# Reordering one stretch of a fused attention and FFN kernel: the halves of the first attended sums ahead of one exponential and one scaling, and a row block's low halves behind a transposition

## The chip, the cores and the metric

The kernel runs on one core of a Trainium2 chip. The metric is device time of one execution in microseconds. A core has several engines that run their own instruction queues side by side: TensorE (PE, matrix products), VectorE (DVE), ScalarE (ACT), GpSimd (POOL) and SyncE (SP, used here to issue DMAs). They wait for one another through semaphores. Within one engine, instructions run in the order in which the compiler queued them.

## The reference

Two branches read the same 2048 x 512 input and are mixed by a gate per row, all in float32.

```python
# attention branch, 32 heads of width 16
q, k, v = split(x @ wqkv)
pq, pk = q @ w_phi[h], k @ w_phi[h]
phi_q = concat(softmax(pq), softmax(-pq))
phi_k = concat(softmax(pk), softmax(-pk))
kv, z = phi_k^T v, sum_s phi_k
a = (phi_q kv) / (phi_q z + 1e-6) @ wo
# feed-forward branch, hidden width 1792
b = relu(x @ w1 + b1)**2 @ w2 + b2
# gate
g = sigmoid(sum(x * gate_w))
out = g * a + (1 - g) * b
```

## The kernel before

Every float32 product is made of three faster ones: each operand is split into a rounded high half and the remainder, its low half, and `mm3` (L74) adds high by high, high by low and low by high. So each operand needs two operations before TensorE can use it: ACT copies it to the high half, and DVE subtracts that from the source to get the low half (`split`, L61; the subtraction is L66 in the profile, the copy L63).

The rows are worked in four blocks of 512, each of four chunks of 128. The feed-forward branch goes over the blocks twice, with one half of the hidden width each time (7 of the 14 tiles). That makes 56 items (`work_list`, L889). An item is an "up" product with its relu, square and split (`up`, `hidden`), and, two items later (`LAG`), the four "down" products that use it (`down`). This stream never ends from the first to the last microsecond, and the attention is fitted between its products: during the first pass over the blocks the keys and values are summed up; during the second the queries are worked, two chunks (a pair) at a time.

The order of the work around the change is written out by hand: `at(slot, f, ...)` puts a step into a slot, and the main loop runs item t with the slots 2t, 2t + 0.5 (in the middle of the up product), 2t + 1 and 2t + 1.5 (in the middle of the down products). The steps of query chunk n are:

- `do_q` (L767): the product q of the chunk on TensorE; then `q_exps` (L361) with `exps` (L329): DVE takes the largest and smallest of each head (mx, mn, L337 and L338) and subtracts them (e, L339 and L340), here called the spread; ACT takes the exponential (L342); DVE sums it (sm, L324) and takes a reciprocal (r, L326); POOL multiplies the exponentials by the normalizers (ez, L367).
- `do_phi` (L770): `q_phi` (L370) sums ez on DVE (dz, L377), works a short chain of small operations (den and w, L378 to L385) and scales the exponentials (`scaled`, L347). `transposed` (L391) transposes the result on DVE (tb, L393) and issues twelve DMAs that carry its pieces to their places in phiT (L403); the other four pieces are copied on ACT (`diagonal`, L409).
- `do_n` (L778) with `numer` (L415): when both chunks of a pair are in phiT, TensorE makes their attended sums (num, L420), and ACT and DVE split those into halves (o).
- `finish` (L811) with `attended` (L441): the product of o with wo (att), added to the row on DVE (L819).

Two means bend the order that the compiler's scheduler gives each engine, which otherwise goes by the place in the program and by what it reckons to be ready. `tc.high_priority(offset=AHEAD)` treats instructions as if they stood 150 places earlier. `tc.issue_after(i)` puts the instructions of the block that run on i's engine behind i in that engine's queue; it does not bind other engines.

`do_x` (L627) with `load_x` (L110) loads and splits a row block of the second pass: the high halves are copied on ACT (xh), the low halves subtracted on DVE (xl). It runs at slot 61 for the block that TensorE first reads in slot 66, and again at slots 72 and 82. Chunk 0 and chunk 1 (the first pair) are worked from slot 56.5 on, chunks 2 and 3 from slot 62.5 on, and the first pair's `do_n` stands at slot 66.5. `do_w1_first` (L505) loads and splits tiles of w1 in the first items, tile 5 at slot 4. Staging tiles of loads (`stage`, four of them) come free when the low half has been taken.

Of the kernel before, what the change touches and what calls it, by code (L numbers as in the profile page):

```python
# [7 lines left out]
F32 = mybir.dt.float32  # L8
# [26 lines left out]
def tile_gated_mix(ctx: ExitStack, tc: tile.TileContext, xT, xn, wqT, wkT, wphi, wv, wo, w1, b1, w2, b2, gw, out):  # L35
# [25 lines left out]
    def split(src, hi, lo, ehi, elo):  # L61
        if ehi is nc.scalar:
            i = nc.scalar.activation(hi, src, AF.Copy)  # L63
        else:
            i = ehi.tensor_copy(hi, src)
        st["lo"] = elo.tensor_tensor(lo, src, hi.bitcast(F32), ALU.subtract)  # L66
        return i
# [16 lines left out]
    def load(src, eng=nc.sync):  # L84
        t = stage.tile([P, 512], F32, tag="in", name="in")
        st["in"] = eng.dma_start(t, src)
        return t
# [4 lines left out]
    def ffn_tiles(nm, fc):  # L92
        return (fpool.tile([P, 512], F32R, tag=nm + "h", name=f"{nm}h{fc}"),
                fpool.tile([P, 512], F32R, tag=nm + "l", name=f"{nm}l{fc}"))
# [4 lines left out]
    def load_ffn(nm, src, fc):  # L99
# [6 lines left out]
        hi, lo = ffn_tiles(nm, fc)  # L106
        st["ffn"] = split(t, hi, lo, nc.scalar, nc.vector)
        return hi, lo

    def load_x(b):  # L110
        xs = []
        for k in range(NK):
            t = load(xT[b, :, k, :])
            hi = xpool.tile([P, SB], F32R, tag="xh", name=f"xh{b}_{k}")
            lo = xpool.tile([P, SB], F32R, tag="xl", name=f"xl{b}_{k}")
            split(t, hi, lo, nc.scalar, nc.vector)
            xs.append((hi, lo))
        return xs

    st, up_w, down_w = {}, {}, {}  # L120
    hold = pool("hold", NV)
# [204 lines left out]
        nc.vector.reciprocal(r, sm)  # L326
        return r

    def exps(ps=None, e=None, late=False):  # L329
        ahead = ps is not None  # L330
        e = e_tile() if ahead else e
        pv = ps.rearrange("p (h f) -> p h f", f=DH) if ahead else e[:, :, 0, :]
        mx = small.tile([P, H], F32, tag="mx", name="mx")
        mn = small.tile([P, H], F32, tag="mn", name="mn")
        bc = lambda t: t.unsqueeze(2).to_broadcast([P, H, DH])
        with tc.high_priority(offset=AHEAD):
            nc.vector.tensor_reduce(mx, pv, AX.X, ALU.max)  # L337
            nc.vector.tensor_reduce(mn, pv, AX.X, ALU.min)  # L338
            nc.vector.tensor_tensor(e[:, :, 1, :], bc(mn), pv, ALU.subtract)  # L339
            nc.vector.tensor_tensor(e[:, :, 0, :], pv, bc(mx), ALU.subtract)  # L340
        ef = e.rearrange("p h t f -> p (h t f)")
        nc.scalar.activation(ef, ef, AF.Exp)  # L342
        e3 = e.rearrange("p h t f -> p (h t) f")
        return e3, None if late else norm(e3)

    def scaled(e3, w):
        nc.vector.tensor_tensor(e3, e3, w.unsqueeze(2).to_broadcast([P, 2 * H, DH]), ALU.mult)  # L347
        return e3.rearrange("p h f -> p (h f)")
# [11 lines left out]

    def q_exps(n, ps):  # L361
        with tc.issue_after(st["den" if n == 1 else "tb"].ins) if n in (1, 2) else nullcontext():
            e3, r = exps(ps, late=n == 3)
        ez = work.tile([P, 2 * H, DH], F32, tag="ez", name="ez", bufs=1)
        for half in range(2):
            hs = slice(half * H, (half + 1) * H)
            st["ez"] = nc.gpsimd.tensor_tensor(ez[:, hs, :], e3[:, hs, :], zbc[half], ALU.mult)  # L367
        st["e", n] = e3, r, ez

    def q_phi(n):  # L370
        e3, r, ez = st.pop(("e", n))
        if r is None:
            with tc.issue_after(st["num"].ins):
                r = norm(e3)
        dz = small.tile([P, 2 * H], F32, tag="dz", name="dz", bufs=2)
        with tc.issue_after(st["num"].ins) if n % 2 and n > 1 else nullcontext():
            nc.vector.tensor_reduce(dz, ez, AX.X, ALU.add)  # L377
        nc.vector.tensor_tensor(dz, dz, r, ALU.mult)  # L378
        d2 = dz.rearrange("p (h t) -> p h t", t=2)
        den = small.tile([P, H], F32, tag="den", name="den", bufs=2)  # L380
        nc.vector.scalar_tensor_tensor(den, d2[:, :, 0], 1e-6, d2[:, :, 1], ALU.add, ALU.add)
        st["den"] = nc.vector.reciprocal(den, den)
        nc.vector.tensor_scalar(den, den, gate[:, n:n + 1], None, ALU.mult)
        w = small.tile([P, H, 2], F32, tag="w", name="w", bufs=2)
        nc.vector.tensor_tensor(w, r.rearrange("p (h t) -> p h t", t=2),  # L385
                                den.unsqueeze(2).to_broadcast([P, H, 2]), ALU.mult)
        return scaled(e3, w.rearrange("p h t -> p (h t)"))

    def transposed(n, phi, pt, u):  # L391
        tb = work.tile([P, 2 * D], F32, tag="tb", name="tb", bufs=2)
        st["tb"] = nc.vector.transpose(tb, phi)  # L393
        later = []
        for j in range(4):
            for r in range(4):
                dst = pt[32 * j:32 * j + 32, u, r, :, :].rearrange("p g s -> p (g s)")
                src = tb[32 * r:32 * r + 32, 256 * j:256 * j + 256]
                if j == r:
                    later.append((dst, src))  # L400
                else:
                    queue = nc.gpsimd if n in (1, NB * NC - 1) and r % 2 else nc.sync
                    st["pieces"] = queue.dma_start(dst, src)  # L403
        return later
# [10 lines left out]
    def numer(pt):  # L415
        pss = [bank(f"num{r}") for r in range(2)]

        def mm(t, q, r):
            rows = slice(64 * r, 64 * r + 64)
            return nc.tensor.matmul(pss[r][32 * q:32 * q + 32, t * 2 * P:(t + 1) * 2 * P], kvb[rows, 4 * t + q, :],  # L420
                                    pt[rows, :, :, 4 * t + q, :].rearrange("p u r s -> p (u r) s"),
                                    start=True, stop=True, skip_group_check=True)


        todo = [(t, q, r) for t in range(2) for q in range(4) for r in range(2)]
        first = mm(*todo[0])
        with tc.issue_after(first.ins):
            second = mm(*todo[1])
        with tc.issue_after(second.ins):
            for x in todo[2:]:  # L430
                mm(*x)
        o = []
        for r in range(2):
            oh, ol = both(work.tile([P, 2 * D], F32R, tag=f"o{r}", name="o", bufs=1))
            with tc.high_priority(offset=AHEAD):
                split(pss[r], oh, ol, nc.scalar, nc.vector)
            st["num"] = st["lo"]
            o.append((oh, ol))
        return o
# [65 lines left out]
    def do_w1_first(fc):  # L505
        with tc.issue_after(st["act0"].ins):
            do_w1(fc)

    def do_w1(fc):
        up_w[fc] = by_k(load_ffn("w1", w1[fc], fc))  # L510
# [114 lines left out]
        st["x", b].append((hi, lo))  # L625

    def do_x(b):  # L627
        with tc.issue_after(st["act"].ins), tc.issue_after(st["pieces0" if b == NB + 2 else "act"].ins):
            st["x", b] = load_x(b % NB)

    ROWS = [divmod(o, 2) for o in (2, 3, 4, 5, 6, 7, 0, 1)]
    LASTP = len(ROWS) - 1
# [59 lines left out]
    def pair_steps(p, s):  # L692
# [45 lines left out]
                place(m, 1, v["Y"], v[5])  # L738

        def phi(t):  # L740
            e3, r = exps(e=v["e", t])
            with tc.high_priority(offset=AHEAD):
                v["phi", t] = scaled(e3, r)

# [24 lines left out]

    def do_phi(b, n, c):  # L770
        with tc.high_priority(offset=AHEAD) if n < 2 else nullcontext():
            phi = q_phi(n)
            if c % 2 == 0:
                st["pt", n // 2] = work.tile([P, 2, 4, NG, 32], F32, tag="phiT", name="phiT", bufs=1)
            st["diag", n] = transposed(n, phi, st["pt", n // 2], c % 2)
        st.setdefault("pieces0" if n % 2 else "", st["pieces"])

    def do_n(pair):  # L778
        st["o", pair] = numer(st["pt", pair])
# [50 lines left out]
    def at(slot, f, *a):  # L830
        steps.setdefault(int(2 * slot) / 2, []).append(lambda: f(*a))

    for fc in range(LAG + 1, NFH):
        if fc > FIRST:
            at(2 * (fc - LAG) - 2, do_w1_first, fc)
        at(2 * (fc - LAG) - (2 if fc == LAG + 1 else 1), do_w2, fc)
    at(0, do_wT, wkT)
    for slot, j, piece in ((5.5, 0, 0), (6, 1, 0), (8, 0, 1), (9, 1, 1), (10, 1, 2), (11, 0, 2)):
# [35 lines left out]
    for p in range(NB * NC // 2):  # L874
        n, s = 2 * p, 56.5 + 6 * p
        q, late = divmod(n, NC)[0], p == NB * NC // 2 - 1
        at(s + 12 - late, finish, n, n % NC)
        at(s + 13 - late, finish, n + 1, n % NC + 1)
        at(s, do_q, NB + q, n, n % NC)
        at(s + 2, do_q, NB + q, n + 1, n % NC + 1)  # L880
        at(s, do_phi, NB + q, n, n % NC)
        at(s + (4.5 if p else 2), do_phi, NB + q, n + 1, n % NC + 1)
        at(s + (5 if p else 4.5), diagonal, n)
        at(s + (7 if p else 6.5), diagonal, n + 1)
        at(s + 10 - late, do_n, p)
    for b, slot in enumerate((5, 2, -2)):
        at((NB + b) * SL + slot, do_x, NB + b + 1)

# [110 lines left out]
```

## Time and profile before

| | |
|---|---|
| median of 3 runs | 509.72 us (509.25 to 510.61) |
| the profiled execution | 511.15 us |
| its span, first to last instruction | 509.3 us |
| mean granted TensorE clock | 0.996 |
| ACT busy, share of the span | 52% |
| HBM traffic | 57.68 MB read, 11.54 MB written |

The profile tells of one execution. The busy time of TensorE counts matmuls that overlap in the pipeline, so one shows 0.39 us though the next starts 0.23 us after it. In a timeline each line gives start and duration in microseconds, the engine, the line of the kernel, the operation, the tile written and those read, the shape and a count; in brackets stands the idle time of the engine just before, and what ended it. A line of the view by windows gives the stretch, its length, the busy time of PE, PEld (weight loads), DVE, ACT and POOL with instruction counts, then the granted clock of TensorE, the share of DMA and GB/s.

### The profile page before, as it was taken

What the parts mean: (1) busy time and instruction counts of PE and PEld (TensorE: products, weight loads), DVE (VectorE), ACT (ScalarE), POOL (GpSimd) and SP (SyncE); (2) the same over time, 40 slices, a digit from 0 to 9 for tenths busy, and PEclk for the clock granted to TensorE, in tenths of its full rate; (3) what the DMA queues carried; (4) which work ended last, traced back from release to release, by engine and by line L of the source; (5) the groups of instructions that cost most, each with busy time, mean ns of one, the idle gap of its engine ahead of it and who ended that gap; (6) DMA issues with size and microseconds to landing.
All of it is one profiled execution on the core that took longest, in us unless ns stands there. A gap on an engine that the chain in (4) does not pass through costs nothing.

```text
span 509.3 us, 9432 instructions
## 1 busy us (share of the span) xinstructions
PE 501.8 (99%) x3520; PEld 404.1 (79%) x3520; DVE 405.6 (80%) x678; ACT 262.9 (52%) x482; POOL 99.5 (20%) x126
## 2 busy tenths in 40 slices
PE   9999999999999999999999989999999999999997
PEld 5878888878888888887888867788787878788776
DVE  5559967898795979797978889897969797897824
ACT  4787745465263474457783644444455344334540
POOL 1000141204420025000332350212222120111310
PEclk9999999999999999999999998999999999999999
DMA  8859597666854578761557131315112231032102
GB/s 264 276 172 302 187 307 214 220 212 223 294 188 161 177 234 300 247 231 60 155 174 252 40 106 43 103 38 170 53 31 86 71 84 43 10 113 74 41 25 82
DMA packets 46174, 77.19 MB, mean 152 GB/s; under 512 B 7148, under 2 KB 22896, under 8 KB 46128
## 3 DMA queue, kind: packets, MB, share of 16 engines
q1 hardware_dynamic: 35584, 41.38, 26.3%
q10 hardware_dynamic: 6768, 23.79, 13.8%
q0 software_dynamic: 3776, 11.41, 6.7%
q8 instruction: 28, 0.46, 0.4%
q14 instruction: 18, 0.15, 0.1%
HBM read 57.68 MB, written 11.54 MB: 136 GB/s over the span
## 4 chain that ended last, share of the span: by engine, by line
PE 81%; DVE 8%; ACT 4%; DMA 3%; POOL 1%; issue 1%; SPq 0%; ACTq 0%; POOLq 0%; DVEq 0%
PE d L76 8%; PE d L77 8%; PE d L78 8%; PE u L76 8%; PE u L77 7%; PE u L78 7%; PE att L78 3%; PE pX L688 3%; PE att L77 3%; PE att L76 3%; PE pX L690 3%; PE pX L689 3%; PE q L76 2%; PE q L78 2%; PE q L77 2%; PE pY L689 2%
## 5 line engine op out<-in xcount | busy, mean ns | idle before, releaser
L456 ACT ACTIVATE r<-u,b1c 128x512 f32<-128x512 f32 x56 | 38.4, 686 | 110.4 <-PE u L78 108.4
L76 PE MATMUL d<-w2h,hh 128*128 128x512 f32 x222 | 86.9, 391 | 0.0
L77 PE MATMUL d<-w2l,hh 128*128 128x512 f32 x222 | 86.4, 389 | 0.0
L78 PE MATMUL d<-w2h,hl 128*128 128x512 f32 x222 | 86.4, 389 | 0.0
L76 PE MATMUL u<-xh,w1h 128*128 128x512 f32 x212 | 83.6, 394 | 0.0
L77 PE MATMUL u<-xl,w1h 128*128 128x512 f32 x212 | 82.6, 390 | 0.0
L78 PE MATMUL u<-xh,w1l 128*128 128x512 f32 x212 | 82.5, 389 | 0.0
L367 POOL TENSOR_TENSOR ez<-e,vext 128x512 f32<-128x512 f32 x32 | 43.3, 1374 | 156.0 <-ACT e L342 156.0
L66 DVE TENSOR_TENSOR hl<-r,hh 128x512 fp32r<-128x512 f32 x56 | 38.3, 686 | 22.8 <-ACT hh L63 22.8
L76 PEld LDWEIGHTS d<-w2h,hh 128*128 128x128 f32 x222 | 41.7, 188 | 10.5 <-issue 1.4
L76 PEld LDWEIGHTS u<-xh,w1h 128*128 128x128 f32 x212 | 39.8, 188 | 11.2 <-issue 2.9
L78 PEld LDWEIGHTS d<-w2h,hl 128*128 128x128 f32 x222 | 41.7, 188 | 8.7
L77 PEld LDWEIGHTS d<-w2l,hh 128*128 128x128 f32 x222 | 41.7, 188 | 8.5
L78 PEld LDWEIGHTS u<-xh,w1l 128*128 128x128 f32 x212 | 39.8, 188 | 8.6 <-DVE w1l L66 0.2
L77 PEld LDWEIGHTS u<-xl,w1h 128*128 128x128 f32 x212 | 39.8, 188 | 8.0
L342 ACT ACTIVATE e<-e 128x1024 f32<-128x1024 f32 x27 | 28.6, 1061 | 33.7 <-DVE e L340 28.4
L324 DVE TENSOR_REDUCE sm<-e 128x64 f32<-128x1024 f32 x27 | 32.8, 1215 | 10.8 <-ACT e L342 10.8
L63 ACT ACTIVATE hh<-r 128x512 fp32r<-128x512 f32 x56 | 35.2, 628 | 1.1
L458 ACT ACTIVATE r<-r 128x512 f32<-128x512 f32 x56 | 35.0, 624 | 0.7
L409 ACT ACTIVATE phiT<-tb 32x256 f32<-32x256 f32 x64 | 26.4, 412 | 9.3 <-DVE tb L393 8.3
L377 DVE TENSOR_REDUCE dz<-ez 128x64 f32<-128x1024 f32 x16 | 19.4, 1215 | 13.0 <-POOL ez L367 13.0
L727 ACT ACTIVATE tmp<-pX 128x512 f32<-128x512 f32 x24 | 14.3, 598 | 29.8 <-PE pX L690 25.9
(190 smaller groups left out, 999.5 us busy)
## 6 DMA issues: line engine op xcount, KB each, us to landing
sloto<-wkeep ACTq DMA_DIRECT2D x30, 512.0 KB, 4.4
in<-in_xT SPq DMA_DIRECT2D x42, 256.0 KB, 4.4
slotez<-wkeep ACTq DMA_DIRECT2D x15, 512.0 KB, 5.2
in<-in_w SPq DMA_DIRECT2D x23, 256.0 KB, 3.5
phiT<-tb SPq DMA_DIRECT2D x180, 32.0 KB, 1.8
part<-row POOLq DMA_DIRECT2D x16, 256.0 KB, 4.8
row<-part SPq DMA_DIRECT2D x16, 256.0 KB, 3.0
out<-row SPq DMA_DIRECT2D x15, 256.0 KB, 2.2
```

Of the source, the lines that this page charges most:

```text
L63: i = nc.scalar.activation(hi, src, AF.Copy)
L66: st["lo"] = elo.tensor_tensor(lo, src, hi.bitcast(F32), ALU.subtract)
L76: nc.tensor.matmul(o, ah[:, sa], bh[:, sb], start=first, stop=False)
L77: nc.tensor.matmul(o, ah[:, sa], bl[:, sb], start=False, stop=False)
L78: return nc.tensor.matmul(o, al[:, sa], bh[:, sb], start=False, stop=last)
L324: nc.vector.tensor_reduce(sm, e3, AX.X, ALU.add)
L342: nc.scalar.activation(ef, ef, AF.Exp)
L367: st["ez"] = nc.gpsimd.tensor_tensor(ez[:, hs, :], e3[:, hs, :], zbc[half], ALU.mult)
L409: nc.scalar.activation(dst, src, AF.Copy)
L456: st["relu"] = nc.scalar.activation(r, ps, AF.Relu, bias=b1c[:, fc:fc + 1])
L458: nc.scalar.activation(r, r, AF.Square)
L689: nc.tensor.matmul(ps, h, wl, start=False, stop=False, skip_group_check=True)
```

## The change

It has four parts.

1. `exps` is cut in two: `spread` (the DVE part up to the subtraction) and `exps` (exponential and sum). For chunk 3, `do_q` does the spread alone; exponential, sum and POOL's product follow in `q_rest` at slot 66.5, behind the first pair's `do_n`. On ACT the exponential is put behind the last high half of the first attended sums (`st["numh"]`).
2. `do_phi` is cut in two: `q_phi` now ends with the weights w, and `do_turn` does the scaling, the transposition and its DMAs. For chunk 2, `do_turn` runs at slot 66.5 too, with the scaling put behind the last low half of the first attended sums (`st["num"]`). For the other chunks both follow directly, as before.
3. `load_x` goes into `do_x`, and the low halves of the row block are put behind chunk 1's transposition on DVE (`st["tb", 1]`). For the blocks at slots 72 and 82 that transposition lies far behind already.
4. Tile 5 of w1 is loaded at slot 4 as before, but split at slot 5, with the high half's copy behind the latest relu on ACT (`do_w1_late`).

The first attended sums' high priority, the DMAs and the arithmetic are unchanged. The diff, with hunks that only rename left out:

```diff
-    def exps(ps=None, e=None, late=False):
+    def spread(ps=None, e=None):
...
             nc.vector.tensor_tensor(e[:, :, 0, :], pv, bc(mx), ALU.subtract)
+        return e
+
+    def exps(e, late=False):
         ef = e.rearrange("p h t f -> p (h t f)")
         nc.scalar.activation(ef, ef, AF.Exp)
...
     def q_exps(n, ps):
         with tc.issue_after(st["den" if n == 1 else "tb"].ins) if n in (1, 2) else nullcontext():
-            e3, r = exps(ps, late=n == 3)
+            e = spread(ps)
+            if n == 3:
+                st["e3"] = e
+            else:
+                q_rest(n, e)
+
+    def q_rest(n, e, after=None):
+        with tc.issue_after(after.ins) if after else nullcontext():
+            e3, r = exps(e, late=n == 3)
...
-        return scaled(e3, w.rearrange("p h t -> p (h t)"))
+        return e3, w.rearrange("p h t -> p (h t)")
...
-                split(pss[r], oh, ol, nc.scalar, nc.vector)
+                st["numh"] = split(pss[r], oh, ol, nc.scalar, nc.vector)
             st["num"] = st["lo"]
...
+    def do_w1_late(fc):
+        hi, lo = ffn_tiles("w1", fc)
+        with tc.issue_after(st["relu"].ins):
+            st["ffn"] = split(st["w1", fc], hi, lo, nc.scalar, nc.vector)
+        up_w[fc] = by_k((hi, lo))
...
     def do_x(b):
-        with tc.issue_after(st["act"].ins), tc.issue_after(st["pieces0" if b == NB + 2 else "act"].ins):
-            st["x", b] = load_x(b % NB)
+        with tc.issue_after(st["act"].ins), tc.issue_after(st["pieces", 1].ins if b == NB + 2 else st["act"].ins):
+            st["x", b] = []
+            for k in range(NK):
+                t = load(xT[b % NB, :, k, :])
+                hi = xpool.tile([P, SB], F32R, tag="xh", name=f"xh{b}_{k}")
+                lo = xpool.tile([P, SB], F32R, tag="xl", name=f"xl{b}_{k}")
+                nc.scalar.activation(hi, t, AF.Copy)
+                with tc.issue_after(st["tb", 1].ins):
+                    nc.vector.tensor_tensor(lo, t, hi.bitcast(F32), ALU.subtract)
+                st["x", b].append((hi, lo))
...
     def do_phi(b, n, c):
         with tc.high_priority(offset=AHEAD) if n < 2 else nullcontext():
-            phi = q_phi(n)
-            if c % 2 == 0:
-                st["pt", n // 2] = work.tile([P, 2, 4, NG, 32], F32, tag="phiT", name="phiT", bufs=1)
-            st["diag", n] = transposed(n, phi, st["pt", n // 2], c % 2)
-        st.setdefault("pieces0" if n % 2 else "", st["pieces"])
+            st["ew"] = q_phi(n)
+            if n != 2:
+                do_turn(n, c)
+
+    def do_turn(n, c):
+        with tc.issue_after(st["num"].ins) if n == 2 else nullcontext():
+            phi = scaled(*st["ew"])
+        if c % 2 == 0:
+            st["pt", n // 2] = work.tile([P, 2, 4, NG, 32], F32, tag="phiT", name="phiT", bufs=1)
+        st["diag", n] = transposed(n, phi, st["pt", n // 2], c % 2)
+        st["tb", n], st["pieces", n] = st["tb"], st["pieces"]
...
-            at(2 * (fc - LAG) - 2, do_w1_first, fc)
+            if fc == 5:
+                at(4, ffn_load, "w1", fc)
+                at(5, do_w1_late, fc)
+            else:
+                at(2 * (fc - LAG) - 2, do_w1_first, fc)
...
         at(s + 10 - late, do_n, p)
+        if p == 1:
+            at(s + 4, lambda: q_rest(3, st["e3"], st["numh"]))
+            at(s + 4, do_turn, 2, 2)
```

More of the change, by code (lines that the diff above doesn't have):

```diff
@@ L108, in load_ffn @@
         return hi, lo
[L110 to L118, printed above, removed]
     st, up_w, down_w = {}, {}, {}
@@ L740, in phi @@
         def phi(t):
-            e3, r = exps(e=v["e", t])
+            e3, r = exps(spread(e=v["e", t]))
             with tc.high_priority(offset=AHEAD):
```

## The prediction

> **What bounds the kernel now.** I read the page first (who is busy), then the waits of TensorE alone, then its timeline around the one long wait, then the other engines there. The first fence is the page's busy line, the second the waits of PE.
>
> ```profile
> PE 501.8 (99%) x3520; PEld 404.1 (79%) x3520; DVE 405.6 (80%) x678; ACT 262.9 (52%) x482; POOL 99.5 (20%) x126
> ```
> ```profile
> PE att L78 <- DVE o L66: 2.2, 1, 2.2
> PE att L76 <- ACT r L456: 0.3, 1, 0.3
> ```
>
> TensorE is busy for 501.8 of 509.3 us, so a change can win only what lies in its gaps and in matmuls run slowly. Nearly all of that lies at one place: the first attended product (att, chunk 0) waits for the low half of `o`. Its timeline, and below it the same stretch one pair later, where nothing waits (columns: start, us, engine, line):
>
> ```profile
> 303.20 0.39 PE L78 MATMUL u<-xh,w1l 128*128 128x512 f32 x1
> 303.91 0.50 PE L76 MATMUL att<-woh,o 128*128 128x512 f32 x1 [0.32 <-ACT r L456]
> 306.80 0.50 PE L78 MATMUL att<-woh,o 128*128 128x512 f32 x1 [2.16 <-DVE o L66]
> 310.69 0.49 PE L76 MATMUL q<-wqh,xh 128*128 128x512 f32 x1
> ...
> 336.30 0.39 PE L78 MATMUL u<-xh,w1l 128*128 128x512 f32 x1
> 336.52 0.39 PE L76 MATMUL att<-woh,o 128*128 128x512 f32 x1
> 336.98 0.39 PE L78 MATMUL att<-woh,o 128*128 128x512 f32 x1
> 339.25 0.39 PE L76 MATMUL q<-wqh,xh 128*128 128x512 f32 x1
> ```
> ```profile
> 304.00:311.00 7.00, 4.84 (x13) 3.52 (x14) 6.90 (x10) 2.81 (x6) 2.02 (x1) 0.76 0.11 28
> ```
>
> From the last u matmul to the first q matmul the disturbed stretch takes 310.69 - 303.20 = 7.49 us, the undisturbed one 339.25 - 336.30 = 2.95. So the wait costs 4.54 us in all, the most that this part of the change can win: 0.32 + 2.16 = 2.48 idle, and 2.06 after it, in which TensorE starts again and runs at a lowered clock (the granted clock over 304 to 311 is 0.76, the windows row above).
>
> The Trainium skill ("TensorE: Matmul & The Clock Gate", the goal table at its end) asks for no idle gaps above about 3 us to keep the clock. By that, a gap of 2.16 us would cost itself alone, and 2.5 us would be the prize. The row with clock 0.76 right behind the gap says otherwise, and I go by the row.
>
> Why the low halves are late (DVE, then ACT, then POOL):
>
> ```profile
> 302.69 2.20 DVE L347 TENSOR_TENSOR e<-e,w 128x1024 f32<-128x1024 f32 x1
> 306.09 1.25 DVE L66 TENSOR_TENSOR o<-num,o 128x512 fp32r<-128x512 f32 x2
> ```
> ```profile
> 301.25 1.06 ACT L342 ACTIVATE e<-e 128x1024 f32<-128x1024 f32 x1 [5.07 <-DVE den L381]
> 302.22 1.06 ACT L63 ACTIVATE o<-num 128x512 fp32r<-128x512 f32 x2
> ```
> ```profile
> 294.43 2.54 POOL L367 TENSOR_TENSOR ez<-e,vext 128x512 f32<-128x512 f32 x2 [0.24 <-ACT e L342]
> 302.45 3.56 POOL L367 TENSOR_TENSOR ez<-e,vext 128x512 f32<-128x512 f32 x2 [5.48 <-ACT e L342]
> ```
>
> ACT stands at the fourth chunk's exponential (chunk 3) from 296 to 301.25, and the copies of `num` (the high halves) queue behind it until 303.28. On DVE the third chunk's (chunk 2) scaling and transposition lie ahead of the low halves, which start at 306.09.
>
> **The change, part by part.**
>
> *Exponential and scaling behind the halves.* The high halves no longer wait for chunk 3's exponential: `num` starts 6.59 us ahead of att where nothing waits (329.93 against 336.52, rows above and below) and takes 1.09, so here, with att due at 303.43, it is done about 297.9. The copies can end at 299 instead of 303.28. The low halves no longer wait for scaling and transposition; the latest place left to them is where the scaling stood, 302.69, and there the first ends by 303.3. The third att matmul would ask for it at 303.20 + 3 x 0.23 = 303.9. So this wait goes, whatever else happens, and the 0.32 with it, since the relu behind the exponential on ACT comes earlier too: 4.54 us gained here. Behind the exponential, which now waits for the copies, stand the relu and POOL's ez; it needs its operand from DVE at 301 anyway, so the new wait holds nothing. Behind the scaling stand chunk 2's transposition, its DMA pieces on SP and four diagonal copies on ACT. Their consumer is the second `num`:
>
> ```profile
> 306.87 15.25 SPq L403 DMA_DIRECT2D phiT<-tb  x23
> ```
> ```profile
> 329.93 1.09 PE L420 MATMUL num<-phiT,kvb 64*32 64x256 f32 x32
> ```
>
> All pieces of chunks 2 and 3 are issued by 322.1; `num`, moved up by 4.54, asks for them at 325.4. That is cover of 3.3 us less a landing, and by the next part the transpositions come no later than now. Nothing is charged.
>
> *Low halves of the row block behind chunk 1's transposition.*
>
> ```profile
> 285.13 0.20 DVE L381 SCALAR_TENSOR_TENSOR den<-dz 128x32 f32<-128x32 f32 x1
> 285.24 0.69 DVE L66 TENSOR_TENSOR xl<-in,xh 128x512 fp32r<-128x512 f32 x1
> ...
> 287.53 0.69 DVE L66 TENSOR_TENSOR xl<-in,xh 128x512 fp32r<-128x512 f32 x1
> 288.13 1.22 DVE L347 TENSOR_TENSOR e<-e,w 128x1024 f32<-128x1024 f32 x1
> 289.38 1.25 DVE L393 STREAM_TRANSPOSE tb<-e 128x1024 f32<-128x1024 f32 x1
> 290.55 0.65 DVE L337 TENSOR_REDUCE mx<-q 128x32 f32<-128x512 f32 x1
> ...
> 292.44 0.68 DVE L340 TENSOR_TENSOR e<-q,mx 128x512 f32<-128x512 f32 x1
> ...
> 294.31 1.22 DVE L324 TENSOR_REDUCE sm<-e 128x64 f32<-128x1024 f32 x1 [0.59 <-ACT e L342]
> 297.01 1.22 DVE L377 TENSOR_REDUCE dz<-ez 128x64 f32<-128x1024 f32 x1 [1.47 <-POOL ez L367]
> 298.61 0.63 DVE L337 TENSOR_REDUCE mx<-q 128x32 f32<-128x512 f32 x1
> ...
> 310.95 0.19 DVE L381 SCALAR_TENSOR_TENSOR den<-dz 128x32 f32<-128x32 f32 x1
> ...
> 312.10 1.23 DVE L347 TENSOR_TENSOR e<-e,w 128x1024 f32<-128x1024 f32 x1
> ```
>
> The four xl stand inside chunk 1's chain of small operations: from den to scaling 288.13 - 285.13 = 3.00 us. The same chain without guests, in chunk 3, takes 312.10 - 310.95 = 1.15. So chunk 1's scaling, its transposition and the spread of chunk 2 (mx to e) come 1.85 us earlier. The xl are four of about 0.60 each, 2.4 us, and need a new place. From the last spread operation to dz(2) pass 297.01 - 292.44 = 4.57 us through ACT and POOL, of which DVE idles 0.59 + 1.47 = 2.06. With everything 1.85 earlier, DVE has from 291.2 to 295.16, that is 3.96 us, for hl (shaped like an xl, 0.6), sm (1.13, its 1.22 less the overlap of neighbours) and four xl (2.4), together 4.13: they overrun by 0.17. dz(2) and all behind it, chunk 3's spread too, then come 1.85 - 0.17 = 1.7 us earlier. The idle time pays for the xl. TensorE needs the first of them here:
>
> ```profile
> 295.61 0.39 PE L77 MATMUL u<-xl,w1h 128*128 128x512 f32 x1
> ```
>
> Directly behind the spread they are done between 291.8 and 293.7, some 2 to 4 us ahead of need.
>
> *What is late next.* Between 296 and 340 DVE has hardly any idle time, so what it does next keeps this lead of 1.7 us. Inside it the low halves only change places with scaling and transposition, so their sum stays. TensorE however comes 4.54 us earlier to the next pair. There the low halves are
>
> ```profile
> 334.77 1.28 DVE L66 TENSOR_TENSOR o<-num,o 128x512 fp32r<-128x512 f32 x2
> ```
>
> The first is done about 335.46 and is asked for at 336.98: slack 1.52. Afterwards it is done at 335.46 - 1.7 = 333.8 and asked for at 336.98 - 4.54 = 332.4. A new wait of 1.3 us stands there. Its size is the unknown cost. It shrinks by up to 1.0 if chunk 2's scaling no longer takes 2.20 us (1.23 where POOL's ez does not run beside it; ez is moved up too, but so is the scaling's neighbourhood, and I expect them to overlap again). It grows if the xl fit worse. I take 1.3, since it follows from the nearest rows; ends 0.3 and 2.3. A pair later there is more room:
>
> ```profile
> 362.44 1.22 DVE L66 TENSOR_TENSOR o<-num,o 128x512 fp32r<-128x512 f32 x2
> ```
> ```profile
> 365.43 0.39 PE L78 MATMUL att<-woh,o 128*128 128x512 f32 x1
> ```
>
> The first is done at 363.1, 2.3 us ahead, and after the new wait TensorE is only 4.54 - 1.3 = 3.2 us earlier and DVE 1.7, so 0.8 is left, and no third wait is charged.
>
> *One w1 tile split later.*
>
> ```profile
> 25.69 0.63 ACT L63 ACTIVATE w1h<-in 128x512 fp32r<-128x512 f32 x1 [2.47 <-DMA in<-in_w]
> 26.23 0.67 ACT L456 ACTIVATE r<-u,b1c 128x512 f32<-128x512 f32 x1
> ```
> ```profile
> 29.58 2.51 DVE L174 STREAM_TRANSPOSE turned<-fold 128x512 f32<-128x512 f32 x4 [0.63 <-PE fold L166]
> ```
> ```profile
> 31.82 0.39 PE L78 MATMUL u<-xh,w1l 128*128 128x512 f32 x1
> ```
>
> Behind the relu, its square and its copy (0.67 + 2 x 0.63) the high half of w1 ends about 28.3 and the low half at 28.9, ahead of the use at 31.82. Nothing is won (TensorE does not wait there) and nothing lost. Only if the low half fell behind the four `turned` would it end at 32.7 and cost 0.9. The load is issued at the same place in SP's queue; a later load that needs its staging tile comes some 2 us later, to data used much later. I take 0.
>
> **The sum.** -4.54 + 1.3 = -3.2 us. The profiled execution's own time is 511.15 us with a span of 509.3; it becomes 507.9 and the span 506.1. The median of the runs shown, 509.72, lies 1.4 below it; what a run is timed at becomes 509.72 - 3.2 = 506.5.
>
> **Rivals.**
>
> *All of it is won.* If DVE gains 3.0 us instead of 1.7 by the second pair (no overlap of ez and scaling, 1.0, and the xl wholly in idle time), the new wait is at most 0.1: 509.72 - 4.54 = 505.2. For it: that idle time exists in the rows. Against: 3.0 is more than the 2.06 idle and the 1.0 together less the 0.17.
>
> *The new wait lowers the clock again.* A wait of 2.16 us did so. If 1.3 is enough, another 2.06 goes: 509.72 - 4.54 + 1.3 + 2.06 = 508.5, within 0.3% of before. The waits of PE name no gap between 0.32 and 2.16 us, so the trace can't tell. By the skill's 3 us (same page) this rival could not occur; the lowered clock at 2.16 makes that a weak argument, so it keeps a chance.
>
> *The other side: the xl go ahead of chunk 2's spread.* Both are let go by the same transposition, and which is first is the scheduler's choice. The spread is marked high priority, which speaks for it, but if its q were not yet counted ready the xl go first. Then the spread starts at 290.55 - 1.85 + 2.4 = 291.1, 0.55 later than now, both DVE waits stay idle, and DVE reaches the second pair 0.55 late instead of 1.7 early. The low half is done at 336.0 for a need at 332.4: a wait of 3.6, longer than the one removed, with its 2.06 of lowered clock. 509.72 - 4.54 + 3.6 + 2.06 = 510.8, slower. It decides once DVE's lead falls below 0.5 us (then wait and clock eat the 4.54).
>
> *The xl come too late.* Behind dz(2) and chunk 3's spread they would end after 299 for the need at 295.61: over 3 us of new wait and the clock with it, some 511 to 512. Their earlier place in the program speaks against it.
>
> **Chances.** Forecast 0.42, all won 0.20, lowered clock again 0.16, xl first 0.12, xl too late or another loss 0.10. Over 0.3% is 1.53 us, about what a measurement of this kernel tells from no change: faster means below 508.2. The forecast and all won are faster, and a part of the lowered-clock case with a shorter wait: 0.42 + 0.20 + 0.07 = 0.69. Same: 0.09 + 0.11 = 0.20. Slower: 0.11. The likeliest case alone reaches from 505.5 (wait 0.3) to 507.5 (wait 2.3 at full clock). The range goes from 504.9, all won and some tenths, to 509.6, so that the lowered clock with a longer wait is in and the two losing cases are mostly out.
>
> **What would show it.** In the changed profile: no wait of att on DVE near 304 and a granted clock of 1.00 there; the copies of num on ACT at 298 to 299, ahead of chunk 3's exponential; the low halves on DVE before the scaling at about 301 to 303; chunk 1's transposition ending near 288.8, mx right behind it and then the four xl; dz(2) near 295.3; the waits of PE naming att <- DVE o once, of about 1.3 us, near 332.4. A wait of u on xl, or xl ahead of mx, would put me on the losing cases. No wait of att anywhere would mean that I undersized DVE's gain; a clock below 1 near 333, that I undersized the second wait's price.

## The result and the profile after

The changed kernel takes 505.94 us (median of 4 runs, 505.19 to 506.69) against 509.55 us for the kernel before (509.25 to 510.61), a ratio of 0.9925 with a 95% interval of 0.9901 to 0.995. That is 3.6 us less; 506.5 us and 3.2 us less were forecast. The profiled execution takes 506.69 us with a span of 504.9, against 511.15 and 509.3: 4.5 us less.

The waits of TensorE in the changed kernel, longest first (total, times, longest in us):

```profile
PE warm L532 <- DVE zeros L526: 1.2, 1, 1.2
PE fold L156 <- issue: 0.6, 1, 0.6
PE pX L703 <- DMA sloto<-wkeep: 0.4, 1, 0.4
```

No att stands there any more, neither the one that waited nor the one a pair later that was feared. Lines have moved: 63, 66 and 78 are the same, the exponential is L335 now, the scaling L340, dz L378, a row addition L840 or L482, the row block's low half L643. TensorE around the first attended product and at the next pair, then the windows row of the same stretch:

```profile
303.38 0.40 PE L78 MATMUL u<-xh,w1l 128*128 128x512 f32 x1
303.61 0.40 PE L76 MATMUL att<-woh,o 128*128 128x512 f32 x1
304.08 0.39 PE L78 MATMUL att<-woh,o 128*128 128x512 f32 x1
306.36 0.39 PE L76 MATMUL q<-wqh,xh 128*128 128x512 f32 x1
...
332.54 0.39 PE L78 MATMUL att<-woh,o 128*128 128x512 f32 x1
```
```profile
303.00:306.40 3.40, 3.40 (x17) 2.79 (x16) 3.40 (x5) 1.61 (x3) 3.40 (x2) 1.00 0.00 0
```

From the last u to the first q it is 306.36 - 303.38 = 2.98 us, where it was 7.49: 4.51 won, at a granted clock of 1.00. The rest of the span differs by a tenth. So this execution won nearly all that the wait and its lowered clock had cost.

The other side, on ACT and DVE:

```profile
298.20 1.09 ACT L63 ACTIVATE o<-num 128x512 fp32r<-128x512 f32 x2 [1.92 <-PE num L421]
301.70 1.06 ACT L335 ACTIVATE e<-e 128x1024 f32<-128x1024 f32 x1 [2.42 <-DVE den L382]
```
```profile
289.57 0.65 DVE L643 TENSOR_TENSOR xl<-in,xh 128x512 fp32r<-128x512 f32 x1
290.14 0.68 DVE L327 TENSOR_REDUCE mx<-q 128x32 f32<-128x512 f32 x1
...
291.34 0.68 DVE L643 TENSOR_TENSOR xl<-in,xh 128x512 fp32r<-128x512 f32 x1
...
293.13 1.28 DVE L643 TENSOR_TENSOR xl<-in,xh 128x512 fp32r<-128x512 f32 x2
...
297.46 1.22 DVE L378 TENSOR_REDUCE dz<-ez 128x64 f32<-128x1024 f32 x1 [1.31 <-POOL ez L368]
...
302.96 1.28 DVE L66 TENSOR_TENSOR o<-num,o 128x512 fp32r<-128x512 f32 x2
304.16 1.22 DVE L340 TENSOR_TENSOR e<-e,w 128x1024 f32<-128x1024 f32 x1
...
318.35 1.22 DVE L314 TENSOR_REDUCE sm<-e 128x64 f32<-128x1024 f32 x1 [0.59 <-ACT e L335]
319.48 0.68 DVE L840 TENSOR_TENSOR row<-att,row 128x512 f32<-128x512 f32 x1
320.08 2.06 DVE L482 SCALAR_TENSOR_TENSOR row<-d,rest,row 128x512 f32<-128x512 f32 x3
...
322.51 1.16 DVE L378 TENSOR_REDUCE dz<-ez 128x64 f32<-128x1024 f32 x1
...
331.38 1.25 DVE L66 TENSOR_TENSOR o<-num,o 128x512 fp32r<-128x512 f32 x2
```

The copies of num (o on ACT) stand ahead of the exponential. The low halves (o on DVE) stand ahead of the scaling, at 302.96, and the first ends 0.44 us before att asks for it at 304.08. Two things were not forecast. The four xl stand around and between the spread's operations (one ahead of mx, one in the middle, two behind), not all behind them. And DVE's queue has another order far behind the edit: four row additions now stand between the sum over chunk 4's exponentials (sm, 318.35) and the sum over POOL's product (dz, 322.51), where the kernel before had DVE idle for 1.47 us; and the next pair's low halves (331.38) have no xl ahead of them. They end in time for the att at 332.54, with 0.5 us to spare. The kernel before has these rows there, with the idle time, the four additions behind dz and the xl:

```profile
321.58 1.22 DVE L377 TENSOR_REDUCE dz<-ez 128x64 f32<-128x1024 f32 x1 [1.47 <-POOL ez L367]
322.72 0.68 DVE L819 TENSOR_TENSOR row<-att,row 128x512 f32<-128x512 f32 x1
...
334.18 0.68 DVE L66 TENSOR_TENSOR xl<-in,xh 128x512 fp32r<-128x512 f32 x1
```

### The profile page after: what moved, and what is told of

The parts are those of the page before. It is cut to its first block, busy times and chain, and to the rows that moved or that the text cites. A ratio compares the mean times of both kernels' runs of the same rounds, so it can differ in the third digit from the quotient of the medians.

```text
span 504.9 us, 9432 instructions
## 1 busy us (share of the span) xinstructions
PE 499.4 (99%) x3520; PEld 402.5 (80%) x3520; DVE 403.2 (80%) x678; ACT 263.6 (52%) x482; POOL 101.8 (20%) x126
## 4 chain that ended last, share of the span: by engine, by line
PE 90%; DVE 3%; DMA 3%; ACT 1%; issue 1%; POOL 0%; POOLq 0%; DVEq 0%; ACTq 0%
PE d L76 9%; PE d L77 9%; PE d L78 9%; PE u L76 9%; PE u L77 9%; PE u L78 9%; PE pX L703 3%; PE att L77 3%; PE att L76 3%; PE q L77 3%; PE q L76 3%; PE att L78 3%; PE q L78 3%; PE pX L705 3%; PE pX L704 3%; PE pY L705 2%
## 5 line engine op out<-in xcount | busy, mean ns | idle before, releaser
L368 POOL TENSOR_TENSOR ez<-e,vext 128x512 f32<-128x512 f32 x32 | 44.7, 1417 | 151.8 <-ACT e L335 151.8
L335 ACT ACTIVATE e<-e 128x1024 f32<-128x1024 f32 x27 | 28.6, 1060 | 33.6 <-DVE e L330 28.3
L378 DVE TENSOR_REDUCE dz<-ez 128x64 f32<-128x1024 f32 x16 | 19.3, 1209 | 11.4 <-POOL ez L368 11.4
```

## The experiments

All edits are shown against the changed kernel. Times are medians; each kernel was run in turn with the kernel before on the same chip.

**The first two parts alone.** The row block and the w1 tile go as before.

```diff
-                with tc.issue_after(st["tb", 1].ins):
+                with nullcontext():
                     nc.vector.tensor_tensor(lo, t, hi.bitcast(F32), ALU.subtract)
...
-            if fc == 5:
+            if fc == 99:
```

> Exponential and scaling behind the first attended sums' halves, nothing else of the change (row block's low halves and the w1 tile as before). Theory A, DVE's order alone decides: low halves ahead of the scaling, and behind them the order that follows from it; then this kernel gains nearly all, 3.5 to 4.4 us, no wait of att on DVE, clock 1.00 near 304. Theory B, the prediction's: the row block's move buys the lead; without it the low halves of the next pair are asked for some 3 us too early, with a lowered clock, and the gain is gone (-1 to +1 us).

It takes 505.12 us against 509.5, ratio 0.9905 (0.9879 to 0.993). The whole gain is there. Its DVE at both pairs, and the two att that ask:

```profile
301.25 1.28 DVE L66 TENSOR_TENSOR o<-num,o 128x512 fp32r<-128x512 f32 x2
...
329.68 1.25 DVE L66 TENSOR_TENSOR o<-num,o 128x512 fp32r<-128x512 f32 x2
```
```profile
302.42 0.39 PE L78 MATMUL att<-woh,o 128*128 128x512 f32 x1
...
330.87 0.39 PE L78 MATMUL att<-woh,o 128*128 128x512 f32 x1
```

Without the row block's move the low halves are still 0.5 us early at both pairs. The prediction had counted on that move for the lead at the second; theory B falls.

**The scaling alone.** The exponential goes back, and so do the two edits of the diff above.

```diff
-            if n == 3:
-                st["e3"] = e
-            else:
-                q_rest(n, e)
+            q_rest(n, e)
...
-            at(s + 4, lambda: q_rest(3, st["e3"], st["numh"]))
```

> Only the scaling and transposition of chunk 2 go behind the low halves; the exponential of chunk 3 stays ahead of the copies on ACT. Theory A: the low halves still come in time (first copy done about 302.8, low half 303.5, due 303.9), so the gain is 3.3 to 4.3 us; at most the 0.3 us wait of att on the relu stays. Rival C, the copies behind the exponential are what is late: att waits again for o, by 0.5 us or more, and the gain is at most half, under 2 us. Theory B: about 0.

505.87 us against 509.5, ratio 0.9932 (0.9908 to 0.9956): 3.6 us of gain. One short wait is left of the old place, for the relu that queues behind exponential and copies on ACT:

```profile
PE att L76 <- ACT r L454: 0.3, 1, 0.3
```
```profile
300.84 1.07 ACT L63 ACTIVATE o<-num 128x512 fp32r<-128x512 f32 x2
```

So the copies, though late on ACT (300.84, against 298.20 in the changed kernel), were not what TensorE waited for long; DVE's order was. The first kernel, which moves the exponential as well, is 0.75 us faster in the median (505.12, with ranges that only touch); 0.3 us of that is the wait shown.

**The exponential alone.** Scaling and transposition go back, and so do the two edits of the first experiment's diff.

```diff
-            if n != 2:
-                do_turn(n, c)
+            do_turn(n, c)
...
-        with tc.issue_after(st["num"].ins) if n == 2 else nullcontext():
+        with nullcontext():
...
-            at(s + 4, do_turn, 2, 2)
```

> Only the exponential of chunk 3 goes behind the copies on ACT; on DVE scaling and transposition stay ahead of the low halves. Theory A: the copies come at 298 to 299, the low halves stay at about 306, the long wait stays at about 2.2 us with its lowered clock: -0.5 to +0.5 us. Rival C: the low halves follow the copies and the gain is over 2 us.

509.42 us against 509.5, ratio 0.9993 (0.9974 to 1.0012): nothing. Its waits, its copies on ACT and its DVE:

```profile
PE att L78 <- DVE o L66: 2.9, 1, 2.9
```
```profile
298.43 1.09 ACT L63 ACTIVATE o<-num 128x512 fp32r<-128x512 f32 x2 [1.73 <-PE num L421]
```
```profile
303.21 2.19 DVE L340 TENSOR_TENSOR e<-e,w 128x1024 f32<-128x1024 f32 x1
...
306.61 1.25 DVE L66 TENSOR_TENSOR o<-num,o 128x512 fp32r<-128x512 f32 x2
```

The copies come early, at 298.43, yet the low halves stay behind the scaling, and rival C falls. DVE's queue was not reordered by an operand that came earlier.

**The row block's low halves alone.** The exponential, the scaling with its transposition and the w1 tile go back.

```diff
-            if n == 3:
-                st["e3"] = e
-            else:
-                q_rest(n, e)
+            q_rest(n, e)
...
-            if n != 2:
-                do_turn(n, c)
+            do_turn(n, c)
...
-        with tc.issue_after(st["num"].ins) if n == 2 else nullcontext():
+        with nullcontext():
...
-            if fc == 5:
+            if fc == 99:
...
-        if p == 1:
-            at(s + 4, lambda: q_rest(3, st["e3"], st["numh"]))
-            at(s + 4, do_turn, 2, 2)
```

> Only the row block's low halves go behind chunk 1's transposition. Theory B: DVE gains a lead of 1.7 us, the wait for the low halves of the first attended sums falls from 2.16 to about 0.5 us and the clock holds: a gain of 3 to 4 us. Theory A, with the lead that the changed kernel's trace shows (dz of chunk 2 at 297.46, none): the wait stays at 2 to 2.5 us: -0.7 to +0.7 us.

509.32 us against 509.5, ratio 0.9987 (0.997 to 1.0004): nothing that can be told from zero.

```profile
PE att L78 <- DVE o L66: 2.1, 1, 2.1
```

**Without the w1 part, without the row block's part, and the changed kernel beside them.** These three and the next ran together. The edits are the two halves of the first experiment's diff: its second for the w1 tile, its first for the row block.

> The changed kernel with the w1 tile split as before; the other three parts stay. Theory A: the w1 part is worth nothing and neither is the row block's part, so this stands within 0.5 us of the changed kernel, run beside it here, and of the kernel with the first two parts alone (505.12 us). Theory B: the row block's part costs or pays over 0.5 us, which shows against the next kernel.

> The changed kernel with the row block's low halves where they stood before; the other three parts stay. Theory A: within 0.5 us of the changed kernel. The prediction's term for this part (DVE 1.7 us late without it) would make the low halves of the next pair late and cost 2 us or more.

> The changed kernel itself, run beside the others of this call as their measure: 505 to 506.7 us by both theories, no wait of att.

They take 505.0 (504.77 to 505.14), 504.8 (504.6 to 505.37) and 505.61 us (504.82 to 505.94), against 509.5; ratios 0.9911, 0.9906 and 0.9921, whose intervals overlap. Neither part shows a gain. The changed kernel has the slowest median of the three, by 0.6 and 0.8 us, a little more than the 0.5 us that was expected; with ranges that overlap this is hinted at, not settled.

**The rows behind the sum.** The order that the prediction had assumed is forced back at one place.

```diff
-            nc.vector.tensor_reduce(dz, ez, AX.X, ALU.add)
+            st["dz", n] = nc.vector.tensor_reduce(dz, ez, AX.X, ALU.add)
...
-        with tc.high_priority(offset=AHEAD):
+        with tc.high_priority(offset=AHEAD), tc.issue_after(st["dz", 4].ins) if n == 1 else nullcontext():
             nc.vector.tensor_tensor(t, ps, t, ALU.add)
...
-                with tc.issue_after(st["dve"].ins) if (sw, b) == (0, NB - 1) else nullcontext():
+                with tc.issue_after(st["dve"].ins) if (sw, b) == (0, NB - 1) else tc.issue_after(st["dz", 4].ins) if (sw, b) == (1, 0) and c else nullcontext():
```

> The changed kernel, but four row additions of DVE (chunk 1's attended row and three rows of the first block's end) go behind the sum over POOL's product of chunk 4, as they stood in the kernel before, in place of ahead of it. If the order that fills DVE's wait for POOL is what kept the next wait away, DVE stands idle for about 1.5 us there, the rows come 1.4 to 2 us late, and a down product waits for its bank by about 1.4 us near 322; with luck of the clock 1.4 us slower than the changed kernel, with a lowered clock 3 us. If DVE had lead enough anyway, no wait and within 0.5 us.

506.6 us against 505.61 for the changed kernel beside it: 1.0 slower (ratios to before 0.9943, 0.9929 to 0.9956, against 0.9921, 0.9907 to 0.9935: the intervals overlap a little). Its DVE, and TensorE:

```profile
316.54 1.22 DVE L314 TENSOR_REDUCE sm<-e 128x64 f32<-128x1024 f32 x1 [0.59 <-ACT e L335]
319.24 1.22 DVE L378 TENSOR_REDUCE dz<-ez 128x64 f32<-128x1024 f32 x1 [1.48 <-POOL ez L368]
320.37 0.68 DVE L840 TENSOR_TENSOR row<-att,row 128x512 f32<-128x512 f32 x1
...
331.15 1.25 DVE L66 TENSOR_TENSOR o<-num,o 128x512 fp32r<-128x512 f32 x2
```
```profile
321.77 0.50 PE L76 MATMUL d<-w2h,hh 128*128 128x512 f32 x1 [0.71 <-DVE row L482]
...
332.45 0.39 PE L78 MATMUL att<-woh,o 128*128 128x512 f32 x1
```

The idle 1.48 us is back, and a down product waits 0.71 us for the bank that a row addition frees. That is half of what was expected, at the place where it was expected. The att of the next pair, where the prediction had put its new wait, still does not wait: the first low half is done about 0.65 us before 332.45. Without the 0.71 that TensorE had already lost it would have been asked for at 331.74, about when it is done. So the filled idle time kept a wait away from the down product; for att it only added to the margin.

**What a late low half costs.** In the kernel with the first two parts alone, the first low half is copied onto itself 2, 3 or 4 times on ACT. This delays TensorE and leaves DVE's order alone.

```diff
                 st["numh"] = split(pss[r], oh, ol, nc.scalar, nc.vector)
+            if r == 0 and "num" not in st:
+                first_low = ol
+            elif r and "again" not in st:
+                st["again"] = True
+                for _ in range(3):
+                    nc.scalar.activation(first_low, first_low, AF.Copy)
```

> The kernel with the first two parts alone (exponential and scaling behind the halves), and in it the first low half of the first attended sums is copied onto itself twice on ACT, so that TensorE gets it later while DVE's and TensorE's orders stay. By that kernel's trace the second copy ends some 1.3 us after the third att matmul asks for it. A clock that falls only after long waits: 1.3 to 1.5 us slower than that kernel's 505.1 in all executions, clock 1.00. A clock that falls already here, as one rival of the prediction had it: part or all of the executions over 3 us slower, with a mean clock of 0.997 or less.

> The same with three copies: a wait of about 2.4 us, near the 2.16 of the kernel before. If the lowered clock hangs on the length of the wait alone, all executions show it and stand 4 to 4.5 us above 505.1. If it hangs on where the wait falls in a window that runs on by itself, some executions show it (4 to 4.5 us) and some don't (2.5 us), as those of the kernel before do: 16 of 26 with a mean clock of 0.997 or less.

> The same with four copies: a wait of about 2.9 to 3.2 us (one q matmul changes its place by the longer wait). Windows that run on by themselves: nearly all executions show the lowered clock, 4.7 to 5.2 us above 505.1. A threshold of the length above 3 us: none, 3 us above.

The waits of att in the three profiles, in this order, are 1.3, 2.0 and 2.4 us (about 2.4 and 2.9 to 3.2 were expected for the last two):

```profile
PE att L78 <- ACT o L443: 1.3, 1, 1.3
```
```profile
304.46 0.50 PE L78 MATMUL att<-woh,o 128*128 128x512 f32 x1 [2.00 <-ACT o L443]
```
```profile
PE att L78 <- ACT o L443: 2.4, 1, 2.4
```

The windows behind the wait, of three copies, of four, and of the kernel before (granted clock: the third number from the end):

```profile
304.50:307.90 3.40, 3.40 (x15) 2.81 (x16) 3.37 (x6) 1.67 (x4) 0.02 (x1) 1.00 0.07 19
```
```profile
306.70:310.00 3.30, 3.30 (x9) 2.58 (x8) 3.16 (x8) 1.18 (x3) 0.00 (x0) 0.50 0.15 40
```
```profile
307.50:310.80 3.30, 3.30 (x10) 2.52 (x9) 3.27 (x5) 1.53 (x4) 0.00 (x0) 0.50 0.21 56
```

Every execution also has a mean clock. It is 0.999 or more, or 0.997 or less; of the three profiles above, that of three copies has 1.000, that of four 0.997 and that of the kernel before 0.996, so I take 0.997 or less as the sign of the lowered clock. The waits are those of the one profiled execution of each kernel. The count of 0.997 or less, by wait: none of 6 at 1.3 us, 5 of 12 at 2.0, 8 of 12 at 2.4; 7 of 12 in the kernel with the row block's part alone (2.1), 7 of 12 in the one with the exponential alone (2.9), and 45 of 58 in the kernel before over the three times it was run (2.2; the first time 17 of 26, one more than the expectation says). The times: 507.2, 508.41 and 509.08 us. With four copies, the executions without the lowered clock have a median of 507.9 and those with it 509.7; with three copies 508.25 and 508.71, so by these medians the price of the lowered clock differs, 1.8 against 0.5 us. Neither theory of the four copies came out whole: 8 of 12 is neither nearly all nor none.

**The row block's low halves where the prediction had put them.** Behind chunk 2's spread, without the w1 part.

```diff
-            nc.vector.tensor_tensor(e[:, :, 0, :], pv, bc(mx), ALU.subtract)
+            st["spread"] = nc.vector.tensor_tensor(e[:, :, 0, :], pv, bc(mx), ALU.subtract)
...
-                with tc.issue_after(st["tb", 1].ins):
+                if b != NB + 1:
                     nc.vector.tensor_tensor(lo, t, hi.bitcast(F32), ALU.subtract)
+                else:
+                    st.setdefault("lows", []).append((lo, t, hi))
...
+    def x_lows():
+        with tc.issue_after(st["spread"].ins):
+            for lo, t, hi in st["lows"]:
+                nc.vector.tensor_tensor(lo, t, hi.bitcast(F32), ALU.subtract)
...
+    at(62.5, x_lows)
```

> The changed kernel without the w1 part, and the row block's low halves behind chunk 2's spread, where the prediction had put them, in place of between its operations. The prediction's step: transposition and spread of chunk 2 then start about 1.85 us earlier against TensorE than in the kernel before and its second sum (dz) about 1.7 us. The time: no wait of TensorE is left to take away, so 504.8 to 505.6 us by all theories.

505.59 us against 510.38 of the kernel before beside it, ratio 0.9911 (0.9893 to 0.993): no wait, as expected. Its trace:

```profile
286.86 0.65 DVE L327 TENSOR_REDUCE mx<-q 128x32 f32<-128x512 f32 x1
...
289.35 1.89 DVE L651 TENSOR_TENSOR xl<-in,xh 128x512 fp32r<-128x512 f32 x3
...
293.69 1.22 DVE L378 TENSOR_REDUCE dz<-ez 128x64 f32<-128x1024 f32 x1 [1.31 <-POOL ez L368]
...
295.28 0.63 DVE L651 TENSOR_TENSOR xl<-in,xh 128x512 fp32r<-128x512 f32 x1
```
```profile
301.28 0.39 PE L78 MATMUL u<-xh,w1l 128*128 128x512 f32 x1
```

Against the u matmul ahead of att, mx stands 14.42 us ahead and dz 7.59. In the kernel before it was 303.20 - 290.55 = 12.65 and 303.20 - 297.01 = 6.19. The leads are 1.8 and 1.4, where 1.85 and 1.7 were reckoned. The lead of mx bears the prediction out. That of dz is near for partly other reasons: only three xl stand behind the spread, the fourth comes behind dz, and DVE still waits 1.31 us for POOL, an idle time that the prediction had spent on the xl.

## Why the prediction was right, and where it was not

*The bound and the removed wait: right, and shown.* TensorE's one long wait was worth 4.54 us in the profiled execution, and 4.51 went. The clock at 304 is 1.00. The cause named, scaling and transposition ahead of the low halves on DVE, is shown by the scaling alone (3.6 us) and the exponential alone (nothing). The prediction gave both edits together the credit. The exponential's removes only the 0.3 us wait on the relu in the traces, and 0.75 us in the medians when the scaling has been moved.

*"DVE keeps this lead of 1.7 us": the term that was mis-sized.* The prediction put the four xl behind the spread. The compiler put two of them between its operations. In the run of the changed kernel beside the others, dz and the u matmul stand as here:

```profile
295.94 1.22 DVE L378 TENSOR_REDUCE dz<-ez 128x64 f32<-128x1024 f32 x1 [1.32 <-POOL ez L368]
...
329.85 1.25 DVE L66 TENSOR_TENSOR o<-num,o 128x512 fp32r<-128x512 f32 x2
```
```profile
302.58 0.39 PE L78 MATMUL u<-xh,w1l 128*128 128x512 f32 x1
```

That is 6.64 us ahead against 6.19: a lead of 0.45, not 1.7. In the profile at the top of this text it is 303.38 - 297.46 = 5.92, no lead at all. Nor was it needed: the kernels without this part are no slower.

*"A new wait of 1.3 us stands there": the step that failed.* The prediction took DVE's order behind the edit as fixed, and read that "between 296 and 340 DVE has hardly any idle time". Neither was so: the trace of the kernel before has the 1.47 us at 320, and the order changed. In the run just shown, from dz to the next pair's low halves DVE takes 329.85 - 295.94 = 33.91 us, in the kernel before 334.77 - 297.01 = 37.76, so 3.85 less. Three items of it are in the rows: the scaling takes 1.22 in place of 2.20 (0.98), the wait for POOL ahead of dz of chunk 4 is filled with row additions (1.47), and no xl stands ahead of the low halves (0.60), 3.05 together; the other 0.8 I have not itemized. With 0.45 + 3.85 = 4.3 us of lead against the 4.54 that TensorE came earlier, the slack of 1.52 at that place was hardly touched. In the profile at the top, without the 0.45, 0.5 us of it is left. With the rows forced back att still did not wait there, nor did it in the kernel with the scaling alone, whose scaling takes 2.12 us; so neither of these two items alone kept the wait away.

The rival that all would be won, at 0.20, is what the profile shows. It named idle time and the scaling's overlap with POOL's ez as the way to it. It argued that 3.0 us of lead was more than there was; it had not counted the second wait for POOL. And the overlap did not go. In the profile at the top ez still covers the scaling, which starts at 304.16:

```profile
302.91 3.63 POOL L368 TENSOR_TENSOR ez<-e,vext 128x512 f32<-128x512 f32 x2 [5.48 <-ACT e L335]
```

In the kernel before, the scaling started at 302.69, within the first of the two ez operations (302.45), and took 2.20. Now the low halves run beside the first ez, the scaling starts as the second is due, and takes 1.22, while the pair of ez still takes 3.63 in place of 2.54 where nothing disturbs it. It looks as if the later of the two waits for the earlier; the rows fit this, no run tests it.

*So the number 506.5 was nearer than its reasons, by luck.* The -4.54 was priced on an execution with the lowered clock. The executions of the kernel before are of both kinds, and those without it lose less by the same wait. In the run with the three kernels side by side, its seven executions with the lowered clock have a median of 509.56, 3.95 above the changed kernel's 505.61, its two others 508.40 and 508.45, 2.8 above. The forecast added a wait that did not come (1.3 us), and took off the full 4.54 of an execution with the lowered clock from a median that holds less of it. The two errors largely offset each other.

*The rival of a clock lowered at 1.3 us: not borne out.* None of six executions with such a wait shows it. The late low half cost 1.6 us there against the kernel of the last experiment, beside which it was run (507.2 against 505.59), and 2.1 against the kernel without the copies (505.12, on another chip). The two rivals on the far side did not occur as described. Of "xl first" a quarter did: one xl stands ahead of mx, which the prediction had named as a sign of losing, but the spread began right behind it and nothing was lost. "Xl too late" did not occur: TensorE did not wait for xl.

*The w1 tile: nothing that can be told from zero, as said.* What DVE's high-priority mark was argued to decide, the place of the xl, it decided only in part.

The kernels without the row block's part, without the w1 part or without both are at least as fast as the changed one; the fastest median, 504.8 us, is that without the row block's part, not separated from the others.

## What to carry to other kernels

On an engine whose queue is fixed, ask first which instruction stands ahead of the one waited for; here bringing its operand earlier changed nothing, and moving the queue's order did. When an edit moves one instruction, look at the whole order that the compiler gives that engine for the next tens of microseconds before you carry a lead or a delay forward: it may fill waits that you took for fixed. And price a stall of TensorE over several executions, since the clock behind it may or may not fall.

## What the runs showed of the hardware

A wait of TensorE of 2.0 to 2.9 us was followed by a lowered clock in some executions and not in others of the same program: 5 of 12 at 2.0 us, 7 of 12 at 2.1, 45 of 58 at 2.2, 8 of 12 at 2.4, 7 of 12 at 2.9, none of 6 at 1.3. Where a profile shows it, the clock is half (0.50 over the 3.30 us of the two windows above). A profile that happens to have the lowered clock overstates the median's gain: 4.5 us by the profiles here, 3.6 by the medians.

The Trainium skill ("TensorE: Matmul & The Clock Gate", Part 1) says that the clock is set by a window of about 3.4 us that runs on by itself, so that the point at which the clock changes depends on where in the window the work falls. The counts above, and the 3.30 us and more at 0.50, agree with that; no run here shows the window itself. The goal table of that page asks for no idle gaps above about 3 us. Here 2.0 us was enough in 5 of 12 executions, and the measurement decides.
